# Batches 1 and 2 of a sliding-window attention: row sums made in 64 rows a head beside the products with v, reciprocals through logarithms, DMA transposes by block

## The chip, the cores and the metric

The kernel runs on one core of a Trainium2 chip. Five engines work side by side, each through its own queue of instructions in order: TensorE (PE), ScalarE (ACT), VectorE (DVE), GpSimd (POOL) and SyncE (SP). The metric is the device time of one execution in microseconds (us), the median of several runs.

## What is computed

Attention with ALiBi biases in a causal window of 128 keys, over 8 batches, 8 heads, 576 positions and 64 values a head; then a gated feed-forward block over the 4608 tokens.

```python
scores = scale * q @ k.T                       # [8, 8, 576, 576], scale 1/8
mask = (rel >= 0) & (rel < 128)                # rel = query position - key position
scores = where(mask, scores - slope[h] * abs(rel), -1e9)
attn = exp(scores - max)
attn = attn / (sum(attn) + 1e-9)
x = (attn @ v)                                 # as 4608 tokens x 512
g = x @ w_gate                                 # 512 x 1536
out = (gelu(g) * (x @ w_val)) @ w_out          # 1536 x 512
```

## The kernel before

The tokens are taken in 9 groups of 512. For each group g, TensorE makes the gate and value products (`gate_val`), then the products with w_out in 16 parts (`out_part`), and between those parts the attention of a later batch: batch g + 2 in general, but batch 1 in the stage of group 0, and batch 2 in that of group 1. The order of each engine's instructions is the order of the program.

Loads from memory go through GpSimd and change f32 to bf16 on the way. q and k of batch 2 and later are then transposed by DMA, issued from SyncE:

```python
qs, ks = [128, 4, 5, 128]      # (position in block, head pair c, block j, two heads of 64)

def load_qk(b):
    for t, src in ((qs[b % 2], q), (ks[b % 2], k)):
        for j in range(5):
            for i in (0, 1):                   # even heads, odd heads
                nc.gpsimd.dma_start(
                    out=t[0:n, :, j, 64 * i:64 * i + 64],
                    in_=src[b][i:H:2, 128 * j:128 * j + n, :].rearrange("c p d -> p c d"))

def transposes_dma(b):
    for src, dst in ((ks, kT), (qs, qT)):
        nc.sync.dma_start_transpose(
            out=dst[b % 2].rearrange("p c (j t) -> p (c j) t", t=128),
            in_=src[b % 2].rearrange("p c j x -> p (c j x)"))
```

`scores` makes the products of k and q in 64x64 pieces, takes exp on ScalarE into P and multiplies with the masked biases on VectorE. Keys lie on 128 partitions, as two halves of 64. The products with v add up over key blocks, even blocks in one half of the partitions and odd ones in the other. Where both halves go to one bank of PSUM, the second half has to begin after the first has ended. This order is made by an empty instruction on SyncE:

```python
def relay(mm):
    by = nc.sync.nop()
    depends(by, mm)                # waits for the last matmul of the first half
    return by                      # the first matmul of the second half waits for it
```

For batches 1 and 2 the sums of P go through TensorE with a matrix of ones into few rows (`sums4`; for the second half of a batch from T, P with overlapping blocks added by VectorE, `add`), then a reciprocal on VectorE, then a product with a selection matrix that spreads the rows over 64 partitions a head, copied by ScalarE (`spread4`). `values` makes the products with v and VectorE multiplies them with those reciprocals into xT:

```python
def sums4(b, s, between=None, added=True):
    # matmuls with ones8, 32 columns; a relay between the halves where T is not used
    nc.vector.reciprocal(row(b)[:, first:first + w], ps[:, 0:w])

def spread4(b, s, copies):
    # 16 matmuls with sel8 on f32, 4 banks
    for g, ps in enumerate(spread4_banks(b, s)):
        copies[g](out=recip[b][...], in_=ps[...])

def values(b, *parts):
    pss = products(b, banks)                   # 64x64 matmuls with vb, with relays
    ...
    nc.vector.tensor_tensor(out=xT[:, c, at:at + e - a], in0=src,
                            in1=recip[b][:, c, a:e], op=ALU.mult)
```

The order of work behind group 0's and group 1's gate products (a number is so many of the 16 output parts):

```python
0: [("s", 1, 0, (0, 1)), 4, ("s", 1, 0, (2, 3)), 2, ("s", 1, 1, (0, 1)), ("add", 1, 1, (0, 1), True), 2,
    ("sum4", 1, 0, lambda: scores(1, 1, (2, 3), masks), False), ("masks",),
    ("add", 1, 1, (2, 3), True), 4,
    ("spread4", 1, 0, acts), ("transposes", 2), 2, ("sum4", 1, 1), ("pv", 1, 0),
    ("spread4", 1, 1, acts), ("pv", 1, 1), 2],
1: [... the same for batch 2, with the scores of batch 3 in between, without ("transposes", ...)]
```

In the later stages the list is `[("table",), 4, ("pv", b - 1), ("s", b, 0, (0,)), 4, ...]`. "table" is an exp of two values, which brings the exponential table into ScalarE. `out_part` issues the store of a finished output tile from SyncE at once, after the copy out of PSUM. Loads and transposes of the next batches are set off so:

```python
for g in range(NG):
    if 1 <= g < B - 2:
        transposes_dma(3 if g == 1 else g + 2)
    if g == 1:
        nc.gpsimd.tensor_copy(out=mark, in_=qT[1][0:1, 0, 0:2])    # GpSimd waits for the transposes
        load_qk(4); load_v(3)
    ... gate_val and steps ...
    if g == 0:
        nc.gpsimd.tensor_copy(out=mark, in_=kT[0][0:1, 0, 0:2])
        load_qk(3); load_v(2)
```

Of the kernel before, what the change touches and what calls it, by code (L numbers as in the profile page):

```python
# [8 lines left out]
BF16 = mybir.dt.bfloat16  # L9
# [18 lines left out]
def kernel(  # L28
# [37 lines left out]
    def keep_busy(ps, n):  # L66
        for _ in range(n):
# [12 lines left out]
    slopes = wo[:, 0:2, :].rearrange("p a (h x) -> p (a h) x", x=128)  # L80
    dist = wo[:, 2, 0:192]
    ones8 = consts.tile([128, 4 * 40], BF16, name="ones8")

    emask = consts.tile([128, H, 448], BF16, name="emask")
    sel0 = consts.tile([128, 8], FP32, name="sel0")
    sel8 = consts.tile([128, 4, 64], FP32, name="sel8")
    mark = consts.tile([1, 2], BF16, name="mark")


    qs, ks = ([consts.tile([128, 4, 5, 128], BF16, name=f"{nm}s{i}") for i in range(2)]  # L90
              for nm in "qk")
    qT, kT = ([consts.tile([128, 4, 640], BF16, name=f"{nm}T{i}") for i in range(2)]
              for nm in "qk")
# [2 lines left out]
    def rows(j):  # L96
        return 64 if j == 4 else 128

    def load_qk(b):
        for t, src in ((qs[b % 2], q), (ks[b % 2], k)):  # L100
            for j in range(5):
                n = rows(j)
                for i in (0, 1):
                    nc.gpsimd.dma_start(  # L104
                        out=t[0:n, :, j, 64 * i:64 * i + 64],
                        in_=src[b][i:H:2, 128 * j:128 * j + n, :].rearrange("c p d -> p c d"))

    def load_v(b, js=range(5)):
        for j in js:
            n = rows(j)  # L110
            nc.gpsimd.dma_start(  # L111
                out=vb[b % 2][0:n, j, :].rearrange("p (h d) -> p h d", h=H),
                in_=v[b][:, 128 * j:128 * j + n, :].rearrange("h p d -> p h d"))

# [1 line left out]

    def runs(what, b, n):
        first, parts, r = RUNS[b][n]  # L120
        t, lo, p = (qs, ks)[what][b].rearrange("p c j x -> p (c j x)"), 1536 * n, 0
        if (b, n) == (0, 1):
            t, lo, p = vb[1].rearrange("p j x -> p (j x)"), 0, 64 * what
        return t[p:p + parts, lo:lo + 512 * r].rearrange("p (h x) -> p h x", h=H)
# [39 lines left out]

    def transposes_dma(b):
        for src, dst in ((ks, kT), (qs, qT)):
            nc.sync.dma_start_transpose(  # L167
                out=dst[b % 2].rearrange("p c (j t) -> p (c j) t", t=128),
                in_=src[b % 2].rearrange("p c j x -> p (c j x)"))


    Ps = [consts.tile([128, H, 896], BF16, name=f"P{i}") for i in range(2)]
# [209 lines left out]

    def products(b, banks):
        pss = [bank() for _ in range(1 + max(u[0] for u in banks))]
        todo, mid = [], 0
        for x in (0, 1):
            at = 0
            for odd in (x, 1 - x):  # L390
                if odd != x:
                    mid = at = max(at, mid)
                wide, small = [], []
                for u, c, lo, hi, to in banks:
                    if u % 2 == odd:
                        (small if hi - lo == 64 else wide).extend(
                            (x, u, c, m, q0, q1, col, to + q0 - lo)
                            for m, q0, q1, col in pieces(b, lo, hi) if m % 2 == x)

                ns, n = len(small), len(small) + len(wide)  # L400
                for k in range(n):
                    t = (small if (k + 1) * ns // n > k * ns // n else wide).pop(0)
                    todo.append((at, *t))
                    at += t[5] - t[4]
        todo.sort()
        begun, by = {}, {}
        for n, (_, x, u, c, m, q0, q1, col, to) in enumerate(todo):
            begun.setdefault(u, x)
            for i in (0, 1):
                h = 2 * c + i  # L410
                mm = nc.tensor.matmul(  # L411
                    out=pss[u][64 * i:64 * i + 64, to:to + q1 - q0],
                    lhsT=vb[b % 2][64 * x:64 * x + 64, m // 2, 64 * h:64 * h + 64],
                    rhs=prob(b)[64 * x:64 * x + 64, c, i, col:col + q1 - q0],
                    start=all(t[2] != u for t in todo[:n]), stop=True, skip_group_check=True)
                if begun[u] != x and u in by:
                    depends(mm, by.pop(u))
            if begun[u] == x and all(t[1:3] != (x, u) for t in todo[n + 1:]):
                by[u] = relay(mm)
        return pss  # L420

    def values(b, *parts):
        if parts:
            banks = [(4 * n + c, c, *part(b, s), 0) for n, s in enumerate(parts) for c in range(4)]
        else:
            banks = [(c, c, 0, 512, 0) for c in (0, 2)] + [(4, c, 512, S, 64 * c) for c in range(4)] + [
                (c, c, 0, 512, 0) for c in (1, 3)]
        pss = products(b, banks)  # L430
        for u, c, lo, hi, to in sorted(banks):
            if u == 4 and hi - lo == 64:
                if c:
                    continue
                c = slice(0, 4)
            a = lo
            while a < hi:
                at = (b * S + a) % RING
                e = min(hi, a + RING - at)
                src = pss[u][:, to + a - lo:to + e - lo] if isinstance(c, int) else (  # L440
                    pss[u][:, 0:256].rearrange("p (c x) -> p c x", c=4))
                nc.vector.tensor_tensor(  # L442
                    out=xT[:, c, at:at + e - a], in0=src, in1=recip[b][:, c, a:e], op=ALU.mult)
                a = e
# [43 lines left out]
    by_dve = {0: (0,), 1: (0,)}  # L488


    done = [0]

    def out_part(g, n):
        for u in range(done[0], done[0] + n):
            t, part = u // 4, u % 4
            if part == 0:
# [5 lines left out]
            if part == 3:  # L502
                osb = o_pool.tile([128, DM], FP32, name="osb")
                (nc.vector.tensor_copy if g < B - 2 and t in by_dve.get(g, (0, 2))  # L504
                 else nc.scalar.copy)(
                    out=osb, in_=acc[g])
                r0 = 512 * g + 128 * t
                nc.sync.dma_start(out=out[r0:r0 + 128, :], in_=osb)
        done[0] = (done[0] + n) % 16

    def out_last(g):
# [17 lines left out]
    raw = [wo[:, 3 + 3 * w:6 + 3 * w, :].rearrange("p a x -> p (a x)").bitcast(FP32)  # L529
           for w in (0, 1)]  # L530

    pairs0 = [t[0].rearrange("p c j x -> p (c j x)")[:, 0:768].rearrange(
        "p (x c y) -> p x c y", x=3, c=2) for t in (qs, ks)]
    pairs1 = wo[:, 9:12, :]
    for h in (0, 2):
# [15 lines left out]
    for h in range(H):  # L551
        nc.vector.memset(slope1[:, h:h + 1], -8.0 * 2.0 ** (-8.0 * (h + 1) / H))
    nc.vector.memset(ones8, 0.0)
    nc.vector.memset(ones8.rearrange("p (h x) -> p h x", x=40)[:, :, 0:8], 1.0)
    nc.vector.tensor_single_scalar(out=ident, in_=tmpl[:, 0:128], scalar=0.0, op=ALU.is_equal)
    for lo, bound, op in ((0, 0.0, ALU.is_lt), (128, 127.5, ALU.is_gt)):
# [131 lines left out]
    nc.gpsimd.memset(T[64:128, :, 0:64], 0.0)  # L688
    nc.gpsimd.memset(Ps[1][:, :, 0:64], 0.0)
    for t in (qs[0], ks[0]):  # L690
        nc.gpsimd.memset(t[64:128, :, 4, :], 0.0)
    load_qk(2)


    acts = (act, act, act, act)
    todo = {
        0: [("s", 1, 0, (0, 1)), 4, ("s", 1, 0, (2, 3)), 2, ("s", 1, 1, (0, 1)), ("add", 1, 1, (0, 1), True), 2,
            ("sum4", 1, 0, lambda: scores(1, 1, (2, 3), masks), False), ("masks",),
            ("add", 1, 1, (2, 3), True), 4,
            ("spread4", 1, 0, acts), ("transposes", 2), 2, ("sum4", 1, 1), ("pv", 1, 0),  # L700
            ("spread4", 1, 1, acts), ("pv", 1, 1), 2],
        1: [("s", 2, 0, (0, 1)), 4, ("s", 2, 0, (2, 3)), 2, ("s", 2, 1, (0, 1)), ("add", 2, 1, (0, 1), True), 2,
            ("sum4", 2, 0, lambda: scores(2, 1, (2, 3), masks), False), ("masks",),
            ("add", 2, 1, (2, 3), True), 4,
            ("spread4", 2, 0, acts), ("s", 3, 0, (0, 1), masks), 2, ("sum4", 2, 1), ("pv", 2, 0),
            ("spread4", 2, 1, acts), ("s", 3, 0, (2, 3), masks), ("pv", 2, 1), 2, ("masks",),
            ("add", 3, 0), ("s", 3, 1, range(4))],
    }

    def steps(g):  # L710
# [14 lines left out]


    def exp_table():
        exp(mark, zeros[0:1, 0:2])

    RUN = {"s": scores, "add": add, "sum4": sums4, "spread4": spread4, "gather": gather, "spread": spread_dma, "pv": values,  # L730
           "masks": flush, "table": exp_table, "transposes": transposes_dma, "last": out_last}

    for g in range(NG):
        if 1 <= g < B - 2:
            transposes_dma(3 if g == 1 else g + 2)
        if g == 1:

            nc.gpsimd.tensor_copy(out=mark, in_=qT[1][0:1, 0, 0:2])
            load_qk(4)
            load_v(3)  # L740
        for f in range(3 if g == 0 else 0, NF):
# [21 lines left out]
        if g == 0:  # L763
            nc.gpsimd.memset(Ps[0][:, :, 0:64], 0.0)
            for t in (qs[1], ks[1]):
                nc.gpsimd.memset(t[64:128, :, 4, :], 0.0)
        for item in steps(g):
            if isinstance(item, int):
                out_part(g, item)
            else:  # L770
                RUN[item[0]](*item[1:])
        if g == 0:

            nc.gpsimd.tensor_copy(out=mark, in_=kT[0][0:1, 0, 0:2])
            load_qk(3)
            load_v(2)

# [29 lines left out]
```

The softmax here doesn't subtract the row's maximum and nothing guards it: scores larger than these inputs give would overflow.

## Time and profile before

| | |
|---|---|
| time, median of 3 runs | 365.58 us (365.37 to 366.13) |
| span of the profiled execution | 363.8 us |
| TensorE busy | 344.4 us (95%) |
| VectorE, ScalarE, GpSimd busy | 196.0, 166.9, 143.3 us |
| mean granted TensorE clock | 0.986 of full |
| loads of q and k, per instruction on GpSimd | 758 and 833 ns mean, 60 each |
| DMA transposes on SyncE | 12, of 3.12 to 5.56 us |

A line of the profile names the engine, the line of the program (L411), the operation, what it writes and reads, and how often; "idle before" is the time for which the engine stood still just ahead of it, and the arrow names what ended that. L411 are the matmuls of `products`, L339 those of `sums4`, L353 those of `spread4`, L470 those of `gate_val`, L499 those of `out_part`; L167 are the DMA transposes, L314 the relays, L104 and L111 the loads of q, k and of v. SPq is SyncE's queue. Ends of matmuls are modelled, so starts are the safer reading.

### The profile page before, as it was taken

To read this page: it belongs to the slowest core of one execution; us is meant where nothing else is said; L and a number is where in the kernel's file an instruction comes from. 1 tells how busy PE (TensorE), PEld (TensorE's weight loads), DVE (VectorE), ACT (ScalarE), POOL (GpSimd) and SP (SyncE) were. 2 spreads that over 40 slices of the span, in tenths; PEclk is the share of its full clock that TensorE was granted. 3 is DMA by queue.
4 is the path that set the end of the run, shared out by engine and by line. 5 is a ranking of instruction groups with operands and counts; after the bars stand their busy time and mean duration, and the time that the engine had idled before them with its cause. 6 is when DMAs were issued, how large, how long until landed. Compare 5 with 4: busy or idle time off the path is not lost.

```text
span 363.8 us, 8340 instructions
## 1 busy us (share of the span) xinstructions
PE 344.4 (95%) x3436; PEld 174.2 (48%) x3436; DVE 196.0 (54%) x359; ACT 166.9 (46%) x328; POOL 143.3 (39%) x202
## 2 busy tenths in 40 slices
PE   8899995399999999999999999999999999999996
PEld 6564542244455445444544454445444544444443
DVE  7883565143486964694469447944694324302420
ACT  6753492143576733743374337433743123323322
POOL 9856486495199007920892089204000000000000
PEclk9999999589999999999999999999999999999999
DMA  9999999999999929997999699979106120011002
GB/s 178 175 196 192 194 133 115 167 117 111 120 134 120 186 48 185 139 163 166 125 143 180 157 116 138 184 167 114 59 31 128 34 82 8 0 59 58 0 29 89
DMA packets 149898, 43.11 MB, mean 119 GB/s; under 512 B 134724, under 2 KB 142820, under 8 KB 149860
## 3 DMA queue, kind: packets, MB, share of 16 engines
q0 software_dynamic: 109440, 18.49, 66.1%
q1 hardware_dynamic: 36976, 17.70, 21.1%
q10 hardware_dynamic: 3444, 6.38, 8.1%
q8 instruction: 27, 0.44, 0.5%
q14 instruction: 11, 0.09, 0.1%
HBM read 43.65 MB, written 9.53 MB: 146 GB/s over the span
## 4 chain that ended last, share of the span: by engine, by line
PE 77%; DMA 7%; ACT 5%; POOL 3%; DVE 3%; SPq 2%; issue 2%; ACTq 0%; POOLq 0%; DVEq 0%
PE ps L470 47%; PE ps L499 20%; DMA wo<-in_moe_w_out_dram 4%; ACT P L186 4%; PE ps L411 3%; PE ps L181 2%; SPq L167 2%; POOL ks L104 2%; PE ps L339 2%; POOL qs L104 2%; DVE osb L504 2%; PE ps L353 1%; DMA ks<-in_k_dram 1%; ACT osb L504 1%; DMA wo<-in_q_dram 1%
## 5 line engine op out<-in xcount | busy, mean ns | idle before, releaser
L477 DVE TENSOR_TENSOR hT<-ps,gelu 128x512 bf16<-128x512 f32 (+3 forms) x112 | 73.5, 668 | 100.9 <-PE ps L470 84.6
L476 ACT ACTIVATE gelu<-ps 128x512 bf16<-128x512 f32 (+3 forms) x112 | 63.6, 581 | 107.1 <-PE ps L470 96.3
L470 PE MATMUL ps<-xT,wg 128*128 128x512 bf16 (+3 forms) x448 | 112.2, 372 | 0.5 <-DVE xT L442 0.3
L470 PE MATMUL ps<-xT,wv 128*128 128x512 bf16 (+3 forms) x448 | 111.6, 372 | 0.0
L499 PE MATMUL ps<-wo,hT 128*128 128x512 bf16 x420 | 96.6, 381 | 0.0
L470 PEld LDWEIGHTS <-wv 128*128 128x128 bf16 x448 | 43.4, 98 | 50.2 <-issue 0.2
L470 PEld LDWEIGHTS <-wg 128*128 128x128 bf16 x448 | 42.8, 98 | 49.7 <-issue 0.7
L186 ACT ACTIVATE P<-ps 128x384 bf16<-128x384 f32 (+2 forms) x128 | 56.1, 542 | 21.2 <-PE ps L181 20.9
L499 PEld LDWEIGHTS <-hT 128*128 128x128 bf16 x420 | 39.2, 98 | 47.1 <-issue 0.7
L104 POOL DMA_DIRECT2D qs<-in_q_dram x60 | 43.1, 758 | 7.8 <-DMA wo<-in_moe_w_out_dram 4.7
L189 DVE TENSOR_TENSOR P<-P,emask 128x768 bf16<-128x768 bf16 (+1 forms) x60 | 34.4, 588 | 18.0 <-ACT P L186 17.8
L104 POOL DMA_DIRECT2D ks<-in_k_dram x60 | 43.5, 833 | 0.0
L111 POOL DMA_DIRECT2D vb<-in_v_dram x40 | 34.5, 963 | 3.6 <-DMA qs<-in_q_dram 1.2
L504 ACT COPY osb<-ps 128x512 f32<-128x512 f32 x25 | 14.7, 588 | 41.9 <-PE ps L499 41.9
L442 DVE TENSOR_TENSOR xT<-ps,rb 128x512 bf16<-128x512 f32 (+3 forms) x49 | 21.7, 509 | 22.0 <-PE ps L411 19.7
L759 POOL COPY mark<-hT 1x2 bf16<-1x2 bf16 x4 | 0.7, 174 | 71.0 <-DVE hT L477 71.0
L411 PE MATMUL ps<-P,vb 64*64 64x192 bf16 (+2 forms) x704 | 18.3, 235 | 10.8 <-SPq L314 10.4
L411 PEld LDWEIGHTS <-vb 64*64 64x64 bf16 x704 | 14.5, 112 | 16.0 <-SPq L314 11.6
L181 PE MATMUL ps<-qT,kT 64*64 64x192 bf16 (+2 forms) x656 | 19.4, 236 | 1.2 <-issue 0.6
L271 DVE TENSOR_TENSOR T<-P 64x1024 bf16<-64x1024 bf16 (+3 forms) x28 | 18.9, 675 | 0.6
L181 PEld LDWEIGHTS <-kT 64*64 64x64 bf16 x656 | 13.1, 106 | 10.1 <-issue 7.7
L344 DVE RECIPROCAL r<-ps 128x128 f32<-128x128 f32 (+3 forms) x16 | 16.1, 1035 | 2.2 <-PE ps L339 2.1
(77 smaller groups left out, 152.6 us busy)
## 6 DMA issues: line engine op xcount, KB each, us to landing
out_dram<-osb SPq DMA_DIRECT2D x35, 256.0 KB
rb<-rd ACTq DMA_DIRECT2D x10, 576.0 KB
vb<-in_v_dram POOLq DMA_DIRECT2D x32, 128.0 KB, 5.0
qs<-in_q_dram POOLq DMA_DIRECT2D x48, 64.0 KB, 3.7
ks<-in_k_dram POOLq DMA_DIRECT2D x48, 64.0 KB, 3.4
wo<-in_moe_w_out_dram POOLq DMA_DIRECT2D x2, 768.0 KB, 14.7
wg<-in_moe_w_gate_dram POOLq DMA_DIRECT2D x5, 256.0 KB, 8.2
wv<-in_moe_w_val_dram POOLq DMA_DIRECT2D x5, 256.0 KB, 8.8
```

The lines of the kernel that those rows point to most:

```text
L104: nc.gpsimd.dma_start(out=t[0:n, :, j, 64 * i:64 * i + 64], in_=src[b][i:H:2, 128 * j:128 * j + n, :].rearrange("c p d -> p c d"))
L111: nc.gpsimd.dma_start(out=vb[b % 2][0:n, j, :].rearrange("p (h d) -> p h d", h=H), in_=v[b][:, 128 * j:128 * j + n, :].rearrange("h p d -> ...
L181: nc.tensor.matmul(out=out, lhsT=kT[b % 2][half, c, 64 * m:64 * m + 64], rhs=qT[b % 2][half, c, q0:q0 + n], start=first, stop=True, skip_g ...
L186: nc.scalar.activation(out=dst, in_=src, func=AF.Exp, scale=0.125)
L189: nc.vector.tensor_tensor(out=dst, in0=dst, in1=m, op=ALU.mult)
L411: mm = nc.tensor.matmul(out=pss[u][64 * i:64 * i + 64, to:to + q1 - q0], lhsT=vb[b % 2][64 * x:64 * x + 64, m // 2, 64 * h:64 * h + 64], r ...
L442: nc.vector.tensor_tensor(out=xT[:, c, at:at + e - a], in0=src, in1=recip[b][:, c, a:e], op=ALU.mult)
L470: nc.tensor.matmul(out=ps, lhsT=w[:, c, 128 * f:128 * (f + 1)], rhs=xT[:, c, t0 + lo:t0 + hi], start=(c == 0), stop=(c == 3))
L476: nc.scalar.activation(out=gl[:, 0:n], in_=pg, func=AF.Gelu)
L477: nc.vector.tensor_tensor(out=hid[g][:, f, lo:hi], in0=pv, in1=gl[:, 0:n], op=ALU.mult)
L499: nc.tensor.matmul(out=acc[g], lhsT=hid[g][:, f, 128 * t:128 * (t + 1)], rhs=wo[:, f, :], start=(f == 0), stop=(f == NF - 1))
L504: (nc.vector.tensor_copy if g < B - 2 and t in by_dve.get(g, (0, 2)) else nc.scalar.copy)(out=osb, in_=acc[g])
```

## The change

For batches 1 and 2 the sums are made by the same routine as the products with v: a matmul with 64 columns of ones gives the sum of a head in all 64 rows that its values occupy, for two or four head pairs at once. No spreading is needed then. The reciprocal is taken on ScalarE as exp(-ln(sum)), with one table that holds both functions, and T, its additions and the selection products go. The order of work in the two stages is new; batch 2's DMA transposes come behind batch 1's products.

q and k are loaded in the layout of v, all 8 heads of a block in one DMA, and each block of 128 positions is transposed by a DMA of its own. A store that would come just ahead of other work on SyncE is kept back until the next output part, or the end of the stage.

```diff
-    qs, ks = ([consts.tile([128, 4, 5, 128], BF16, name=f"{nm}s{i}") for i in range(2)]
+    qs, ks = ([consts.tile([128, 5, DM], BF16, name=f"{nm}s{i}") for i in range(2)]
...
+    def load(t, src, b, js=range(5)):
         for j in js:
             n = rows(j)
             nc.gpsimd.dma_start(
-                out=vb[b % 2][0:n, j, :].rearrange("p (h d) -> p h d", h=H),
-                in_=v[b][:, 128 * j:128 * j + n, :].rearrange("h p d -> p h d"))
+                out=t[0:n, j, :].rearrange("p (h d) -> p h d", h=H),
+                in_=src[b][:, 128 * j:128 * j + n, :].rearrange("h p d -> p h d"))
+    def load_qk(b):
+        load(qs[b % 2], q, b)
+        load(ks[b % 2], k, b)
...
     def transposes_dma(b):
         for src, dst in ((ks, kT), (qs, qT)):
-            nc.sync.dma_start_transpose(
-                out=dst[b % 2].rearrange("p c (j t) -> p (c j) t", t=128),
-                in_=src[b % 2].rearrange("p c j x -> p (c j x)"))
+            for j in range(5):
+                nc.sync.dma_start_transpose(
+                    out=dst[b % 2][:, :, 128 * j:128 * j + 128], in_=src[b % 2][:, j, :])
...
+    def values_and_sums(b, s):
+        row(b)
+        lo, hi = ((0, 256), (256, 512))[s]
+        banks = [(n, slice(2 * n, 2 * n + 2), lo, hi, 0) for n in (0, 1)] + [
+            (2 + c // 2, c, lo, hi, 256 * (c % 2)) for c in range(4)]
+        if s:
+            banks += [(4, slice(0, 4), 512, S, 0)] + [
+                (4, c, 512, S, 256 + 64 * c) for c in range(4)]
+        pss = products(b, banks)               # a slice of c: sums, with ones64
+        two = [...]                            # n = 1, then n = 0, then the last 64 queries
+        for c, a, e, sums, _ in two:
+            nc.scalar.activation(out=recip[b][:, c, a:e], in_=sums, func=AF.Ln)
+            nc.scalar.activation(out=recip[b][:, c, a:e], in_=recip[b][:, c, a:e], func=AF.Exp, scale=-1.0)
+        for c, a, e, _, prods in two:
+            at = b * S + a
+            nc.vector.tensor_tensor(
+                out=xT[:, c, at:at + e - a], in0=prods, in1=recip[b][:, c, a:e], op=ALU.mult)
...
     def out_part(g, n):
+        store()                                # what was kept back
...
-                nc.sync.dma_start(out=out[r0:r0 + 128, :], in_=osb)
+                stores.append(dict(out=out[r0:r0 + 128, :], in_=osb))
+                if g >= B - 1 or u + 1 < done[0] + n:
+                    store()
...
-        0: [("s", 1, 0, (0, 1)), 4, ... ("spread4", 1, 0, acts), ("transposes", 2), 2, ("sum4", 1, 1), ("pv", 1, 0),
-            ("spread4", 1, 1, acts), ("pv", 1, 1), 2],
-        1: [("s", 2, 0, (0, 1)), 4, ... ("pv", 2, 1), 2, ("masks",), ("add", 3, 0), ("s", 3, 1, range(4))],
+        0: [("table",), ("s", 1, 0, (0, 1)), 4, ("s", 1, 0, (2, 3)), 2, ("s", 1, 1, (0, 1)), 2, ("s", 1, 1, (2, 3)), ("pv+", 1, 0), 4, ("pv+", 1, 1), ("transposes", 2), 4],
+        1: [("table",), ("s", 2, 0, (0, 1)), 3, ("s", 2, 0, (2, 3)), 2, ("s", 2, 1, (0, 1)), 2, ("s", 2, 1, (2, 3)), ("pv+", 2, 0), 3, ("pv+", 2, 1), 1, ("s", 3, 0, (0, 1)), 2, ("s", 3, 0, (2, 3)), 3, ("add", 3, 0), ("s", 3, 1, range(4))],
...
     def exp_table():
-        exp(mark, zeros[0:1, 0:2])
+        nc.scalar.preload_act_table_set("natural_log_exp_and_others")
...
-            nc.gpsimd.tensor_copy(out=mark, in_=qT[1][0:1, 0, 0:2])
+            nc.gpsimd.tensor_copy(out=mark, in_=qT[1][0:1, 0, 512:514])
...
+        store()                                # at the end of a group's steps
         if g == 0:
-            nc.gpsimd.tensor_copy(out=mark, in_=kT[0][0:1, 0, 0:2])
+            nc.gpsimd.tensor_copy(out=mark, in_=kT[0][0:1, 0, 512:514])
```

## The prediction

> **What bounds the kernel now.** I read the busy shares first. TensorE (PE) is busy 344.4 us of a span of 363.8, so 19.4 us of the span are open to a change like this one, apart from TensorE work that it takes away. Then the table by stage, which says where those 19.4 us lie (columns: stretch in us, its length, PE busy time and count, granted clock, DMA share, GB/s).
>
> ```profile
> 0.00:28.40 28.40, 24.81 (x548) 1.00 1.51 184
> 28.40:57.00 28.60, 28.29 (x314) 1.00 1.60 173
> 57.00:75.70 18.70, 9.17 (x150) 0.73 1.10 129
> 75.70:96.40 20.70, 20.70 (x101) 1.00 1.52 136
> 96.40:118.40 22.00, 20.93 (x393) 1.00 1.22 109
> 139.10:155.00 15.90, 15.60 (x222) 1.00 1.51 148
> 155.00:175.40 20.40, 20.40 (x125) 1.00 1.21 165
> ```
>
> The gate and value products (75.7 to 96.4, 155.0 to 175.4) have no gap. The opening 28.4 us lack 3.6 us, which the change does not touch. Half of all that is missing lies in 57.0 to 75.7: 9.5 us of idle PE, at a clock of 0.73. This is the end of the stage that prepares batch 1, so I read the timeline there:
>
> ```profile
> 59.49 0.46 PE L411 MATMUL ps<-P,vb 64*64 64x192 bf16 x16
> ...
> 63.01 3.12 SPq L167 DMA_TRANSPOSE kT<-ks  x1
> 66.19 3.12 SPq L167 DMA_TRANSPOSE qT<-qs  x1
> 68.15 0.17 POOL L774 COPY mark<-kT 1x2 bf16<-1x2 bf16 x1 [7.56 <-DMA kT<-ks]
> ...
> 69.49 0.74 PE L411 MATMUL ps<-P,vb 64*64 64x192 bf16 x16 [9.53 <-SPq L314]
> ```
>
> The first 16 products with v end at 59.95; the next 16 start at 69.49, and they wait for SPq L314, the empty instruction on SyncE (the `relay`) that lets the second half of a bank begin after the first. It does nothing itself, but SyncE takes its queue in order, and ahead of it the item ("transposes", 2) has put the two DMA transposes of batch 2. The chain of waits shows what those waited for:
>
> ```profile
> 58.25 4.56 DMA ks<-in_k_dram
> ...
> 63.01 3.12 SPq L167
> 66.13 0.06 issue
> 66.19 3.12 SPq L167
> ```
>
> GpSimd issues the loads of batch 2 until 58.25, the last one lands at 62.81, the two transposes take SyncE until 69.31. So batch 1's products wait for batch 2's loads, through a queue that they merely share. The stall costs twice: the granted clock is 0.50 from 69.4 until 74 or later (0.62 for 74 to 75). The 95 matmuls from 69.45 to 75.71 take 6.26 us at a mean clock of 0.58, so about 6.26 x 0.58 = 3.6 us at full clock: 2.6 us more. The stall is thus worth 9.5 + 2.6 = 12.1 us.
>
> The same wait exists in small elsewhere:
>
> ```profile
> PE ps L411 <- SPq L314: 0.9, 4, 0.2
> PE ps L353 <- DVE r L344: 0.5, 1, 0.5
> PE ps L339 <- SPq L314: 0.3, 1, 0.3
> ```
>
> That is everything after 75 us: four relays, 0.22 us each, in the stages of groups 2 to 5, where the relay stands behind the store of an output tile (SPq L508), itself waiting for a copy; and about a microsecond of waits in the stage of batch 2.
>
> **What the Trainium skill says.** *TensorE: Matmul & The Clock Gate*, Part 1: after an idle window of about 3.4 us the clock goes to half, and comes back after about as much sustained work. The trace agrees in kind: half clock after 9.5 us of idling, full again some 5 us after work resumed. *ScalarE: Activation LUTs*, "Table sets: the hidden batching unit": natural_log_exp_and_others holds exp and ln together, so alternating them needs no reload; its section on ACT_TABLE_LOAD gives about 1283 ns, and 186 ns + 0.833 ns per element for an ACTIVATE. Here every load is 1283 ns and a 128x512 copy out of PSUM 588 ns (the formula: 613). No Ln occurs before the change. *DMA: Bandwidth & Descriptors*, "Rules for kernel authors": coalesce small transfers. Here a load of q or k carries 64 KB and takes GpSimd 0.72 us (ten in 7.20 us), one of v 128 KB in 0.87 us (five in 4.37). *Perfetto Trace Analysis*, on HWDGE DMA instructions: their recorded time ends before the data has moved. Here the kT transpose leaves SyncE at 66.13 and its reader gets it at 68.15.
>
> **The change, part by part.**
>
> *1. The relays come free of the transposes.* ("transposes", 2) moves behind both halves of batch 1's products. The 12.1 us should go nearly whole: the inputs of these products are batch 1's, all present.
>
> *2. Sums.* Removed per batch: ones8 sums (24+24 and 16 matmuls; start to start 0.45 + 0.45 + 0.39 us in the stage of batch 2), spread4 (0.65 + 1.13 us, waits included) and the old products with their relays (1.39 + 2.6 us, of which about 0.4 are scores of batch 3). Sum about 6.7 us of PE's path. Added: values_and_sums. First half, queries 0 to 256: 4 key blocks of widths 192, 192, 128, 64; 32 value matmuls and 16 sum matmuls, the latter two head pairs wide. Second half: six key blocks for 256 to 512 and three for the rest, so 72 value and 24 + 6 sum matmuls. A full batch of 88 value products takes about 1.95 us (142.55 to 144.5), 22 ns each: 104 make 2.3 us. The 46 wide ones cost 28 ns if issue bounds them (1.3 us), or as much as the values if columns do (2.4 us), since the columns are equal. I take 4.6 us with relays at 0.2 to 0.4, about 5.0. So PE gains 1.3 to 2 us per batch, less what new waits give back. In batch 1 most of the waits removed are already in the 12.1 us; I count 0.5 there, 1.3 in batch 2.
>
> *3. ScalarE and VectorE.* Added to ScalarE per batch: 4 Ln and 4 Exp on 128x512 (about 0.6 us) and one of each on 128x256 (0.39): 5.6 us. Removed: 8 copies of spread4, 4 x 0.30 + 4 x 0.35 = 2.6 us. Net +3.0 us. VectorE loses the T adds and copies (3.4 us) and two reciprocals (0.96 + 1.16 us). ScalarE is busy 15.98 of 22.07 us in batch 2's stage, so it goes to about 19 of 21. It is not the bound, but it is nearly full. In the second half the chain is Ln, Exp, Ln, Exp (2.4 us), then a multiply (0.68): 3.1 us. The sums are ready about 1 us before the last value product, and 12 output matmuls (2.7 us) follow before the next group reads xT: it fits in batch 1 with about 0.5 us to spare. In batch 2 more work follows, but the Ln and Exp stand ahead of batch 3's exponentials, which hold the banks that the last scores want: I take 0.3 to 0.8 us of PE waiting there, already taken off in the 1.3.
>
> *4. Loads and transposes.* 10 loads of 128 KB at 0.87 us replace 20 of 64 KB at 0.72: GpSimd needs 8.7 us a batch, not 14.5. The DMA queues are full anyway around 45 us, so batch 2 lands at about 55 instead of 62.8. The transposes turn from 2 of 20 blocks (3.12 us, 0.156 us a block) into 10 of 4 blocks: 0.62 us if proportional; I allow 0.65 to 0.8, so 6.5 to 8 us a batch instead of 6.2. SyncE reaches them after the last relay of batch 1, about 60, and is through at 67 to 68. Then GpSimd may load batch 3 (its marker waits for kT alone, about 65.5): issued by 75, landed by 79, transposed by about 86. Batch 2's relays stand behind those transposes, and PE gets to them at about 62.8 + 20.7 + 6.9 = 90.4. This is hidden, with 4 us to spare.
>
> *5. Stores.* A store that would stand ahead of a relay is held until after: up to 4 x 0.22 = 0.9 us.
>
> *6. Table.* The preload replaces a dummy exponential: 0.2 us less on ScalarE in four stages, none on the path.
>
> Sum: 12.1 + 0.5 + 1.3 + 0.9 = 14.8 us. 365.58 - 14.8 = 350.8; call it **351.0 us**.
>
> **Rivals.**
>
> *A. The wait moves to batch 2.* If a small transpose has a fixed cost of 1.5 to 2 us on SyncE, ten take 15 to 20 us. Then batch 3 is transposed not at 86 but at 97 or later, and the relays of batch 2 wait 6 us or more, and the clock drops again: 358 to 362 us. For it: the order in SyncE's queue is the very one that caused today's stall, and the transposes have taken up to 5.6 us when loads ran beside them. Against it: two transposes follow each other with 0.06 us between, and a store of 256 KB holds SyncE only 0.33 us, so no large fixed cost shows.
>
> *B. ScalarE becomes the bound of stages 0 and 1.* About 3 us more per stage, with sums and exponentials in one queue, could hold PSUM banks and delay xT at the start of the next group: 1 to 3 us lost in each, 353 to 356 us. For it: the 19 of 21 us above. Against it: in batch 1's stage ScalarE stood idle for most of 12.64 us, and PE work covers the chain.
>
> *C. The stall was hiding another.* With PE 12 us earlier, a later load comes too late (v of batch 2, or q and k of batch 4). I reckon v of batch 2 landed by 84, needed at 90; batch 4 needed only 40 us later. This would cost a few us.
>
> *D. The sums run at 28 ns or less and no bank waits:* 349 us.
>
> **Range and chances.** Part 1 is nearly certain, because it is an order in a queue and nothing else fills that stretch. The uncertainty is A (about 1 in 8, adding 3 to 10 us) and B (1 in 4, adding 1 to 4), and D on the other side. Hence 348.5 to 355.0. Two per cent faster means under 358.3; only a bad A reaches that: faster 0.93, same 0.05, slower 0.02.
>
> **What would show each step.** Right: no PE gap over 1 us between 45 and 62, clock 1.00 throughout, next group's gate products starting at 62 to 64 instead of 75.7; SPq L314 gone from PE's waits; DMA_TRANSPOSE at 0.6 to 0.8 us times 60 on SyncE; loads of q and k at about 0.87 us; ACT with Ln at about 0.6 us and no table load between Ln and Exp. Wrong: a long PE wait for SPq L314 in batch 2's stage (A); PE waiting for ACT at the first gate products of groups 1 and 2 (B); PE waiting for loads or kT (C). The steady stages should change by 0.2 us each, hardly more.

## The result and the profile after

| | before | after |
|---|---|---|
| time, median | 365.48 us (364.87 to 366.13) | 355.57 us (354.75 to 357.35) |
| ratio, 95% interval | | 0.9735 (0.9692 to 0.9778) |
| TensorE busy / span of the profiled execution | 344.4 / 363.8 us | 341.0 / 354.3 us |
| idle TensorE in the span | 19.4 us | 13.3 us |

The change is 2.7% faster. 351.0 us had been predicted, with 355.0 as the upper end; it is 4.6 us slower than the prediction and 0.6 us outside the range. The table by stage of the kernel after shows where (stretch, its length, PE busy, granted clock, DMA share, GB/s):

```profile
45.60:62.60 17.00, 16.99 (x305) 1.00 1.51 133
62.60:83.40 20.80, 20.80 (x100) 1.00 1.37 137
83.40:110.80 27.40, 22.10 (x359) 0.88 1.63 146
110.80:132.40 21.60, 21.58 (x129) 1.00 0.85 143
```

Batch 1's stage (45.6 to 62.6) has lost its gap and ends at 62.6, where the prediction had 62 to 64. But batch 2's stage (83.4 to 110.8) takes 27.4 us, where it took 22.07, and has a clock of 0.88. In the list of PE's waits after, the relays stand first; before, they cost 9.5 us in batch 1's stage and 0.9 in the later ones:

```profile
PE ps L419 <- SPq L312: 5.0, 2, 4.8
PE ps L179 <- issue: 1.2, 1, 1.2
PE ps L68 <- DVE zeros L567: 1.0, 1, 1.0
```

L312 is the relay again, L419 the matmuls of `products`. It is the old stall in another stage, half as long. The timeline there:

```profile
80.67 6.87 SPq L166 DMA_TRANSPOSE kT<-ks  x5
87.60 7.54 SPq L166 DMA_TRANSPOSE qT<-qs  x5
95.23 15.44 SPq L527 DMA_DIRECT2D out_dram<-osb  x4
```
```profile
90.25 0.86 PE L419 MATMUL ps<-P,vb 64*64 64x192 bf16 x16
...
95.96 0.19 PEld L419 LDWEIGHTS <-ones 64*64 64x64 bf16 x8 [5.04 <-SPq L312]
95.96 0.74 PE L419 MATMUL ps<-P,ones 64*64 64x384 bf16 x8 [4.85 <-SPq L312]
...
96.39 0.84 PE L419 MATMUL ps<-P,vb 64*64 64x192 bf16 x16
96.55 0.17 POOL L770 COPY mark<-qT 1x2 bf16<-1x2 bf16 x1 [13.73 <-DMA qT<-qs]
```

PE's first half of batch 2's products ends at 91.1. The relay stands on SyncE behind the ten DMA transposes of batch 3 (80.67 to 95.14) and one store. They had been expected to be over at 86. The table by stage, cut finer, shows the clock after the gap:

```profile
96.00:97.00 1.00, 1.00 (x24) 0.50 0.70 260
...
101.00:102.00 1.00, 1.00 (x24) 0.55 1.86 199
102.00:103.00 1.00, 1.00 (x54) 1.00 1.68 236
```

One line of the detail of L166 gives the time for which one transpose holds SyncE (min/median/max in ns):

```profile
L166 SPq DMA_TRANSPOSE kT<-ks x30: 1188/1206/2321, 59.1 to 225.2; - x30
```

A transpose of 4 blocks takes 1.19 us at the least, where 0.65 to 0.8 had been allowed. The other half of the delay stands in GpSimd's timeline, at the marker that lets batch 3's loads go:

```profile
68.27 0.17 POOL L807 COPY mark<-kT 1x2 bf16<-1x2 bf16 x1 [14.49 <-DMA kT<-ks]
68.72 4.20 POOL L102 DMA_DIRECT2D qs<-in_q_dram  x5 [0.28 <-issue]
72.86 4.24 POOL L102 DMA_DIRECT2D ks<-in_k_dram  x5
```

GpSimd has waited 14.49 us for batch 2's kT, so batch 3's loads start at 68.7; the first kT transpose of batch 3, which needs the first block of k, begins only at 80.67, after SyncE has waited 6.0 us for the load of k.

### The profile page after: what moved, and what is told of

The parts are those of the page before. It is cut to its first block, busy times and chain, and to the rows that moved or that the text cites. A ratio compares the mean times of both kernels' runs of the same rounds, so it can differ in the third digit from the quotient of the medians.

```text
span 354.3 us, 8217 instructions
## 1 busy us (share of the span) xinstructions
PE 341.0 (96%) x3368; PEld 171.1 (48%) x3368; DVE 186.4 (53%) x333; ACT 171.6 (48%) x328; POOL 107.4 (30%) x143
## 4 chain that ended last, share of the span: by engine, by line
PE 85%; ACT 6%; SPq 3%; DVE 2%; issue 2%; DMA 1%; ACTq 0%; DVEq 0%
PE ps L501 53%; PE ps L537 21%; PE ps L419 5%; ACT P L184 4%; SPq L166 3%; PE ps L179 2%; PE ps L337 1%; ACT osb L542 1%; DMA wo<-in_q_dram 1%; DVE osb L542 1%; PE ps L144 1%; PE ps L555 1%; PE ps L351 1%; ACT rb L445 0%; ACT rb L446 0%
## 5 line engine op out<-in xcount | busy, mean ns | idle before, releaser
L537 PE MATMUL ps<-wo,hT 128*128 128x512 bf16 x420 | 98.0, 385 | 0.0
L542 ACT COPY osb<-ps 128x512 f32<-128x512 f32 x25 | 14.7, 590 | 34.1 <-PE ps L537 34.1
L102 POOL DMA_DIRECT2D qs<-in_q_dram x30 | 25.2, 858 | 6.4 <-DMA wo<-in_moe_w_out_dram 4.4
L102 POOL DMA_DIRECT2D ks<-in_k_dram x30 | 25.4, 898 | 0.0
L473 DVE TENSOR_TENSOR xT<-ps,rb 128x512 bf16<-128x512 f32 (+3 forms) x33 | 15.5, 536 | 6.7 <-PE ps L419 6.7
L419 PE MATMUL ps<-P,vb 64*64 64x192 bf16 (+2 forms) x736 | 17.9, 224 | 0.2
L419 PEld LDWEIGHTS <-vb 64*64 64x64 bf16 x736 | 15.0, 109 | 4.1 <-issue 2.7
L269 DVE TENSOR_TENSOR T<-P 64x1024 bf16<-64x1024 bf16 (+1 forms) x20 | 15.0, 752 | 0.4
L449 DVE TENSOR_TENSOR xT<-ps,rb 128x512 bf16<-128x512 f32 (+1 forms) x10 | 6.4, 638 | 14.4 <-ACT rb L446 14.3
## 6 DMA issues: line engine op xcount, KB each, us to landing
wo<-in_moe_w_out_dram POOLq DMA_DIRECT2D x2, 768.0 KB, 14.7
```

Source lines behind the costliest of these rows:

```text
L102: nc.gpsimd.dma_start(out=t[0:n, j, :].rearrange("p (h d) -> p h d", h=H), in_=src[b][:, 128 * j:128 * j + n, :].rearrange("h p d -> p h d"))
L269: nc.vector.tensor_tensor(out=to[half, :, 2 * n0 + x:2 * n1 + x - 1:2], in0=P[half, :, 3 * n0:3 * n1 - 2:3], in1=P[half, :, 3 * n0 + 1:3 * ...
L419: mm = nc.tensor.matmul(out=out, lhsT=lhsT, rhs=prob(b)[half, c, i, col:col + q1 - q0], start=all(t[2] != u for t in todo[:n]), stop=True, ...
L537: nc.tensor.matmul(out=acc[g], lhsT=hid[g][:, f, 128 * t:128 * (t + 1)], rhs=wo[:, f, :], start=(f == 0), stop=(f == NF - 1))
```

## Experiments

Two theories were tested. **Queue**: batch 3's transposes are late (they start late, through the marker, and cost 1.2 us each), and batch 2's relays stand behind them on SyncE; the stall and the half clock are the whole shortfall. **ScalarE**: the logarithms and exponentials, 3 us more per stage, hold the banks of PSUM and delay xT, and the relay merely comes last.

### The relays on VectorE

```diff
-        by = nc.sync.nop()
+        by = nc.vector.nop()
```

> The changed kernel, with the relays as empty instructions on VectorE instead of SyncE; transposes, loads and all else unchanged. Theory (SyncE's queue: the ten transposes of batch 3 stand ahead of batch 2's relays): the wait of 4.8 us and the half clock after it go, though the relays now stand behind the masks of the last scores and may wait up to 1.5 us; 347.5 to 349.5 us. Rival (ScalarE, with its logarithms and exponentials, or late data bounds this stage): 354 to 356 us, the gap stays under another name.

Measured: 351.44 us, ratio to the kernel before 0.9614 (0.9576 to 0.9652). The clock stays at 1.00 throughout the profiled execution. SyncE's transposes are as long as before, and PE does not wait for them. It waits for the relays in VectorE's queue now:

```profile
PE ps L419 <- DVEq L312: 2.5, 2, 1.5
```

4.1 us come back, less than the 6 to 8 expected: the relays now stand behind VectorE's masks, and PE waits for them for 1.5 us in batch 1's stage and 1.0 in batch 2's. ScalarE's work was unchanged in this run, so the second theory does not explain the stall; SyncE's queue does. The queue held things up in both directions, though. Batch 2's transposes, no longer behind batch 1's relays, start at 53.88 instead of 59.15; the marker is released at 62.78 instead of 68.27; and batch 3's transposes are over at 88.31 instead of 95.14, before PE comes to the relay (92.2):

```profile
74.08 7.37 SPq L166 DMA_TRANSPOSE kT<-ks  x5
81.50 6.81 SPq L166 DMA_TRANSPOSE qT<-qs  x5
```

### The marker left out

```diff
         if g == 0:
-            nc.gpsimd.tensor_copy(out=mark, in_=kT[0][0:1, 0, 512:514])
             load_qk(3)
```

> The changed kernel without the marker that holds GpSimd's loads of batch 3 until kT of batch 2 has been transposed; the loads go to buffers that are free, so nothing else has to wait. If the late start of these loads is what makes batch 3's transposes late: they start at about 75 instead of 80.7, right behind the stores, end at about 88, batch 2's relays (91) are free, 347.5 to 349.5 us. If it is the cost of the ten transposes alone, and they get slower still beside the loads (over 1.6 us each): 352 us or more. Rival (ScalarE): 354 to 356 us.

Measured: 349.23 us, ratio 0.9548 (0.9504 to 0.9592). The 6.3 us against the kernel after are the shortfall and a little more. Batch 3's loads start at 53.7 instead of 68.7. In the timeline of this run its transposes still cost what they did, and end in time:

```profile
58.90 6.90 SPq L166 DMA_TRANSPOSE kT<-ks  x5
65.84 9.38 SPq L166 DMA_TRANSPOSE qT<-qs  x5
75.31 1.00 SPq L527 DMA_DIRECT2D out_dram<-osb  x2
76.42 6.50 SPq L166 DMA_TRANSPOSE kT<-ks  x5
82.97 7.46 SPq L166 DMA_TRANSPOSE qT<-qs  x5
```

They are over at 90.43; the relay waits 0.39 us instead of 4.85, batch 2's stage takes 20.26 us (83.09 to 103.35), and no clock is lost. The queue theory's second expectation, transposes so slow beside the loads that they still come late, did not happen, though the qT of batch 2 took 9.38 us beside them. There is no slack, however: from 58.90 to 90.43 SyncE goes from one transpose or store to the next, and 30.2 of these 31.5 us are transposes. The relay's wait of 0.39 us stands behind the last of them and one store.

### The loads and transposes of before

The layout, 20 loads of 64 KB and two transposes of 20 blocks a batch come back; all else is changed.

```diff
...
-            for j in range(5):
-                nc.sync.dma_start_transpose(
-                    out=dst[b % 2][:, :, 128 * j:128 * j + 128], in_=src[b % 2][:, j, :])
+            nc.sync.dma_start_transpose(
+                out=dst[b % 2].rearrange("p c (j t) -> p (c j) t", t=128),
+                in_=src[b % 2].rearrange("p c j x -> p (c j x)"))
```

> The changed kernel with the loads and transposes of before (20 loads of 64 KB, two transposes of 20 blocks a batch), all else changed. If the fixed cost of small transposes is the whole cause: no wait for a relay in batch 2's stage, 348 us. If late loads share in it: loads issued by about 83, transposes from about 84 to 93 or 95, so the relays of batch 2 (91) still wait 2 to 4 us, and 350 to 355 us. Rival (ScalarE): 354 to 356 us.

Measured: 358.29 us, ratio 0.9786 (0.9744 to 0.9828). This is more than the 350 to 355 us expected for late loads. The relay's wait, expected at 2 to 4 us, grows to 6.3 (L111 are the loads, L170 the transposes in this kernel):

```profile
70.40 7.18 POOL L111 DMA_DIRECT2D qs<-in_q_dram  x10 [0.28 <-issue]
77.48 7.27 POOL L111 DMA_DIRECT2D ks<-in_k_dram  x10
```
```profile
87.10 5.90 SPq L170 DMA_TRANSPOSE kT<-ks  x1
93.05 5.07 SPq L170 DMA_TRANSPOSE qT<-qs  x1
```

So the many small transposes are not the only road to the stall. With few large transposes SyncE needs 11 us a batch instead of 14.5, but the smaller loads take GpSimd 14.2 us instead of 8.4, and the transposes start 6.4 us later. As long as the marker holds the loads back, batch 2's relays are late either way. The loads of 128 KB are a gain here, which the small transposes partly eat.

### The same, without the marker

> The kernel with the loads and transposes of before and all else changed (358.3 us), now also without the marker. If its wait of 6.3 us came from the late start of batch 3's loads: loads issued by about 77, transposes over by 88 to 91, wait gone or under 1 us, 349 to 351.5 us, so the small loads and the size of the transposes hardly matter once the loads start early. If the slower loads still bind: 353 us or more.

Measured: 351.11 us, ratio 0.9620 (0.9583 to 0.9656): the relay's wait is gone, and 7.2 us with it. Started early enough, the old loads and transposes do nearly as well as the new ones (349.23; the two intervals overlap). Their transposes are over at 90.17, and PE comes to the relay at 92.7, so this queue has slack where that of the new transposes has none.

### The kernel before, with the transposes moved

```diff
-            ("spread4", 1, 0, acts), ("transposes", 2), 2, ("sum4", 1, 1), ("pv", 1, 0),
-            ("spread4", 1, 1, acts), ("pv", 1, 1), 2],
+            ("spread4", 1, 0, acts), 2, ("sum4", 1, 1), ("pv", 1, 0),
+            ("spread4", 1, 1, acts), ("pv", 1, 1), ("transposes", 2), 2],
```

> The kernel before, with the item of batch 2's transposes moved behind both halves of batch 1's products, and nothing else. If the order in SyncE's queue was the whole of the old stall: 353 to 354 us. But batch 3's transposes then end at about 95 as before, and batch 2's first relay comes to PE at about 92: with a wait of about 3 us there it is 356 to 358 us. If the stall comes from the data and not from the order: 365 us.

Measured: 359.75 us, ratio 0.9831 (0.9794 to 0.9868). The old stall vanishes: group 1's gate products start at 65.41 instead of 75.55. But this order alone brings the stall into the next stage:

```profile
93.59 0.58 PE L181 MATMUL ps<-qT,kT 64*64 64x192 bf16 x24
96.54 0.83 PE L339 MATMUL ps<-P,ones 64*32 64x64 bf16 x24 [2.36 <-SPq L314]
```

A wait of about 3 us had been expected, and 2.4 came. The time lies 2 us above the expected 356 to 358; the clock fell to half in this short gap too, for 6.8 us, which is worth about 3 us and had not been reckoned with.

### The sums of before, without the marker

The two lists of steps of before (with the transposes behind batch 1's products), all else as in the run of 349.23 us.

> The changed kernel without the marker (as in the run without it, 349.2 us), and with the sums of before: ones8 sums, VectorE reciprocals, spreading by sel8, in the order of work of before with the transposes behind batch 1's products. This takes the new sums alone out. If they save PE what was reckoned (1.3 to 2 us a batch, and relay waits): 352.5 to 354.5 us. Rival (ScalarE's added 3 us a batch cost what the sums save on PE): 349 to 350 us. A relay wait at batch 2's sums, which come earlier than its products, would add to it: up to 357.

Measured: 354.59 us, ratio 0.9698 (0.9665 to 0.9731). The new sums, together with their order of work, which this run does not separate from them, are worth 5.4 us in two stages, more than the 1.3 to 2 us a batch that were reckoned on PE. In this run's waits (L337 is `sums4`, L351 `spread4`) stand 1.1 us for T (VectorE's additions) and 1.1 us for reciprocals, none of which the new sums have:

```profile
PE ps L337 <- DVE T L273: 1.1, 2, 0.8
PE ps L351 <- DVE r L342: 1.1, 3, 0.5
```

### Reciprocals on VectorE, without the marker

```diff
-            nc.scalar.activation(out=recip[b][:, c, a:e], in_=sums, func=AF.Ln)
-            nc.scalar.activation(out=recip[b][:, c, a:e], in_=recip[b][:, c, a:e], func=AF.Exp, scale=-1.0)
+            nc.vector.reciprocal(recip[b][:, c, a:e], sums)
```

> As the run without the marker (349.2 us), but the reciprocals by VectorE straight from the sums, four of 128x512 and one of 128x256 a batch, instead of Ln and Exp on ScalarE. Reciprocals of 128x160 took 1.11 us and of 128x128 0.95, so 5 ns an element more: about 2.9 us for 512. If that chain of 2.9 us each holds xT and the banks: VectorE +13 us a batch, 353 to 358 us. If the logarithms on ScalarE were what limits these stages: 346 to 348 us.

Measured: 370.13 us, ratio 1.0136 (1.0094 to 1.0177), slower than the kernel before and above the expected 353 to 358 us.

```profile
L445 DVE RECIPROCAL rb<-ps 128x512 f32<-128x512 f32 x8 | 26.2, 3323 | 0.8 <-PE ps L419 0.8
L445 DVE RECIPROCAL rb<-ps 128x256 f32<-128x256 f32 x2 | 3.4, 1695 | 0.0
```

In the kernel after, Exp and Ln do the same step on ScalarE:

```profile
L446 ACT ACTIVATE rb<-rb 128x512 f32<-128x512 f32 x8 | 5.0, 630 | 0.3
L445 ACT ACTIVATE rb<-ps 128x512 f32<-128x512 f32 x8 | 4.8, 600 | 9.3 <-PE ps L419 9.3
```

PE's waits without Ln and Exp (L500 are the gate products, L536 the output parts):

```profile
PE ps L500 <- DVE xT L448: 7.6, 1, 7.6
PE ps L419 <- DVE rb L445: 5.7, 3, 2.7
PE ps L536 <- DVE rb L445: 1.4, 1, 1.4
```

A reciprocal of 128x512 takes 3.32 us, Ln and Exp together 1.23. PE waits 14.7 us in all for VectorE, and the clock falls to half twice, which the expectation had not counted. With its sum in all 64 rows of a head, each reciprocal is made 64 times over: 2304 columns of 128 partitions a batch, where the kernel before had 288. Between the two engines tried, ScalarE is the one on which this pays. ScalarE is thus a part of the change that the new sums need, and not their limit.

### Stores not held back, without the marker

```diff
-                if g >= B - 1 or u + 1 < done[0] + n:
+                if True:
```

> As the run without the marker (349.2 us), but every store is issued at once as before. If the relays of the later stages wait behind the stores for 0.22 us as the waits of before show: 350 us (+0.9); if the whole difference of the steady period (36.36 us before, 35.97 after) comes from it: 350.8 us (+1.6) or a little more with the two stages of batches 1 and 2. Rival (stores do not matter): 349.2 us.

Measured: 350.60 us, ratio 0.9599 (0.9568 to 0.9629). The difference of 1.4 us to the run with held stores is inside the two intervals, but the period of the later stages shows it in one profile of each: the chain (the work that ended last, followed back from the end) has `out_part` of these stages start at 125.27, 161.62, 197.98, 234.32 and 270.67, so every 36.35 us as in the kernel before (140.03, 176.39, ...), and every 35.97 us where stores are held (124.95, 160.92, 196.88, ...). 0.38 us in each of four periods make 1.5 us, about as much as the two times differ.

### Transposes of half a block

The kernel after, marker in place, with 20 transposes of 2 blocks a batch.

```diff
             for j in range(5):
-                nc.sync.dma_start_transpose(
-                    out=dst[b % 2][:, :, 128 * j:128 * j + 128], in_=src[b % 2][:, j, :])
+                for c in (0, 2):
+                    nc.sync.dma_start_transpose(
+                        out=dst[b % 2][:, c:c + 2, 128 * j:128 * j + 128],
+                        in_=src[b % 2][:, j, 128 * c:128 * c + 256])
```

> The changed kernel (355.6 us, marker in place) with each block's transpose cut in two: 20 DMA transposes of 2 blocks a batch. If a small transpose has a fixed cost of about 1.2 us on SyncE: 24 to 28 us a batch, batch 2's relays wait 12 to 18 us more, 368 to 376 us. If the 1.2 us is made up of the data moved (0.3 us a block): 0.6 us each, the same 12 to 14 us a batch, and about 356 us.

Measured: 407.82 us, ratio 1.1157 (1.1100 to 1.1214).

L421 are the products with v in this kernel, L314 the relay, L503 the gate products:

```profile
L167 SPq DMA_TRANSPOSE kT<-ks x60: 1167/1196/2063, 58.6 to 273.7; - x60
```
```profile
PE ps L503 <- ACT gelu L509: 24.1, 4, 7.9
PE ps L421 <- SPq L314: 21.1, 1, 21.1
```

Half the data take the same 1.2 us, so at this size it is a cost per transpose. The relay waits 21.1 us, 16 more than in the kernel after. The time is above the expected 368 to 376 us, and the later stages stall too (24.1 us), which had not been expected. In the chain, ScalarE's own DMA of the sums in those stages begins just when the last qT has landed, and the Gelus stand behind it in ScalarE's queue; no run tests this.

### Transposes of 5 and of 10 blocks

The kernel with old loads and without the marker, with each tensor's transpose in four or in two pieces.

> As the run before in this call, with each tensor's transpose as four DMA transposes of 5 blocks instead of one of 20. It measures the cost by size. If the cost is a floor of about 1.2 us with 0.156 us a block hidden under it: 1.2 us each, 9.7 us a batch. If it is 1.2 us fixed plus 0.1 us a block or so: 1.7 us each, 14 us a batch. If proportional: 0.8 us each.

> The same with two DMA transposes of 10 blocks a tensor. Floor: max(1.2, 1.56) = 1.6 us each. Fixed plus a part by size, as 1.2 us at 4 blocks and 3.12 at 20 would make it on a straight line (0.73 + 0.12 a block): 1.9 us each.

Timed once each: 349.07 and 348.01 us, too few to compare. The transposes of k took:

```profile
L171 SPq DMA_TRANSPOSE kT<-ks x24: 1201/1243/2592, 61.1 to 217.8; - x24
```
```profile
L171 SPq DMA_TRANSPOSE kT<-ks x12: 1441/2469/3388, 61.4 to 215.2; - x12
```

The smallest time of such a transpose for 2, 4, 5, 10 and 20 blocks is 1.17, 1.19, 1.20, 1.44 and 3.12 us: flat up to 5 blocks, and over the whole neither proportional nor a straight line. Up to 5 blocks that is the floor of the first expectation; 10 come out even under its 1.6. The medians of the large ones are well above (2.5 us for 10, 5.1 for 20 in the kernel before). Loads run beside many of them; how much of the difference is theirs, no run here separates.

### More copies on VectorE, without the marker

```diff
-    by_dve = {0: (0,), 1: (0,)}
+    by_dve = {0: (0, 2), 1: (0, 2, 3)}
```

> As the run without the marker (349.2 us), with one more output copy in batch 1's stage and two more in batch 2's on VectorE instead of ScalarE. If ScalarE holds the banks of batch 3's last scores in batch 2's stage (PE waits there about 0.4 us for a copy and some exponentials): 348.3 to 349 us. If ScalarE does not limit any stage: 349.2 us, or more where the copies come behind masks on VectorE.

Measured: 348.88 us, ratio 0.9562 (0.9530 to 0.9594), not to be told from 349.23 (0.9548). Easing ScalarE brings nothing that can be measured, so its load did not bound these stages.

## Why the prediction was wrong

**The step that failed** is the fourth: "The transposes turn from 2 of 20 blocks (3.12 us, 0.156 us a block) into 10 of 4 blocks: 0.62 us if proportional; I allow 0.65 to 0.8, so 6.5 to 8 us a batch instead of 6.2." The term is mis-sized by nearly two: a transpose held SyncE for 1.2 us at the least, and the ten of a batch for 14.3 to 14.5 us. I took the rate of a long transfer for the cost of a short one, and argued from the 0.06 us between two transposes that nothing is fixed. A gap between instructions cannot show a cost inside them.

What followed, against the steps of the prediction: the marker was released at 68.27, not 65.5 (kT of batch 2 took 7.72 us on SyncE instead of 3.3 to 4). The loads were issued by 77.1, not 75. The first k block came to its transpose at 80.67, 7.8 us after its issue, so "landed by 79" was too early as well: the loads of k in this stretch took 7.8 us from issue to landing in the median, where those of the kernel before took 3.4 over the whole span. The transposes then ended at 95.14, not 86. The 4 us to spare became a wait of 4.85, which is 4.5 more than without the marker, and the half clock cost about 3 us more (96.0 to 101.9 at half). These 7.5 us are about what batch 2's stage was longer than without the marker: 7.2 (27.48 against 20.26). That the result is only 4.6 us off is in part luck, since the other steps together gave more than predicted: without this stall the kernel takes 349.23 us, 1.8 less than predicted.

**Rival A came true**, with 1 chance in 8: the queue, a cost that each small transpose has, and the clock. Its sizes were too large: 1.2 us a transpose and not 1.5 to 2, an end at 95.1 and not at 97 or later, 355.57 us and not 358 to 362. It is not the whole cause either, as two large transposes a batch brought the stall too (6.3 us) while the marker held the loads back. The case against it, the 0.33 us of a store, compared two kinds of DMA; no small transpose stood in the profile before.

**What was right or merely off:**

- Step 1: the old stall goes whole. Batch 1's stage shrank from 29.92 us (45.63 to 75.55) to 16.38 (46.15 to 62.53), so by 13.5, of 12.6 predicted with its share of the sums.
- Step 2 was reckoned too small. values_and_sums takes 1.37 + 2.18 us of PE's path (53.66 to 55.03, 57.72 to 59.90), not 5.0. That is 150 matmuls at 24 ns, near the lower end of its reckoning, where the wide sums cost 28 ns and not twice as much. With their order of work the new sums are worth 5.4 us, not 1.8.
- Step 3: Ln 0.60 and Exp 0.63 us as reckoned, no table load between them. ScalarE is busy 18.48 of 20.26 us in batch 2's stage without the stall and still costs PE no wait over 0.2 us, though it is close: the chain of that run follows ScalarE from 95.7 to 103.3. Rival B falls, by the runs with the relays on VectorE and with more copies there. The chain in batch 1 fits: the last multiply of the first 512 queries ends just as the gate products start.
- Step 5: the held stores bring 0.38 us a stage instead of 0.22, 1.5 us in all.
- Rival C: batch 2's v was in time. Rival D had the sums right (28 ns a wide one, no bank waits). Its time, 349 us, came only with an edit that it did not have, the marker left out: the 14.8 us were 16.3 with the new stall taken out.

What stays open is how much the cost per transpose alone did with the loads of 128 KB, since whole transposes in the new layout were not run. An estimate: begun at 80.67 and taking the 11.0 us of the run with the old loads, they would end at 91.7, 0.6 us after PE comes to the relay. Open is also why PE's first scores of batch 1 start 0.5 us later in the profile of the kernel after (46.15). The 0.5 us stand in one wait of the opening for nothing that the profile names: 1.22 us before 18.51, against 0.65 in the kernel before and 0.63 in the run with the relays on VectorE.

## What to carry to other kernels

When a wait is taken off a shared queue, follow every later user of that queue with the new times: what the stall delayed now meets what used to be over. Take the cost of a small transfer from a small transfer of its own kind, not from the rate of a large one. A marker that paces loads should be looked at again when compute moves forward: leaving it out brought 349.23 us here, and of the kernels timed more than once only one was faster, by 0.35 us, which is inside the noise.

## What the runs showed of the hardware that had not been expected

- A DMA transpose of k issued from SyncE held it for at least 1.17 to 1.20 us for 2, 4 and 5 blocks of 128x128 in bf16, 1.44 for 10, 3.12 for 20.
- The clock fell to half in a PE gap of only 2.4 us (94.2 to 96.5, in the kernel before with the transposes moved), and stayed there for 6.8 us. The Trainium skill, *TensorE: Matmul & The Clock Gate*, Part 1, says that the clock goes to half after at least one idle window of about 3.4 us; here the whole gap was shorter than that. The mean clocks of 0.97 from 95 to 96 in this run and of 0.91 from 91 to 96 in the kernel after put the fall 1.8 us into this gap and 4.0 us into that of the kernel after:

```profile
95.00:96.00 1.00, 0.00 (x0) 0.97 1.28 290
96.00:97.00 1.00, 0.46 (x20) 0.50 0.63 211
...
102.00:103.00 1.00, 1.00 (x14) 0.61 1.31 83
```

- VectorE's reciprocal takes 6.4 ns for each further element of a row ((3323 - 1695) / 256, from 128x512 and 128x256). The 5 ns of the expectation came from two close sizes (128 and 160) alone; the smallest and the largest of the kernel before, 96 and 192, give (1358 - 758) / 96 = 6.3.
